# From the third expert on, the scaled routing weights are loaded and multiplied instead of multiplied and transposed

## The chip, the cores and the metric

The kernel runs on one core of one Trainium2 chip. The metric is the device time of one execution in microseconds (us). The median of three runs of the kernel before is 1072.27 us (1066.41 to 1077.67).

## What is computed

Three layers follow each other: an attention (pooled and local, added), a soft mixture of experts, and a second mixture of experts with a balanced gate. The change lies in the passage from the second to the third.

```python
# soft mixture: logits = x @ phi; slot_out comes from 8 experts with 4 slots each
c = exp(logits - logits.max(1)); c /= c.sum(1) + 1e-09
x = c @ slot_out                      # 2304 tokens x 512, from 32 slots
# second mixture, x is the x above
P = exp(x @ w_gate - max)             # 2304 x 8
for _ in range(8):                    # balanced by rows and by columns
    P /= P.sum(1, keepdims=True) + 1e-09
    P /= P.sum(0, keepdims=True) + 1e-09
    P *= N / E
out = 0
for e in range(E):                    # 8 experts, D=512, F=1024
    h = maximum(x @ w1[e], 0.0)
    out += P[:, e:e + 1] * (h @ w2[e])
```

Since x is c @ slot_out, x @ w1[e] is c @ (slot_out @ w1[e]), a product over 32 slots alone. And since P is positive, P * max(h, 0) is max(P * h, 0), so the gate of an expert can be multiplied into c before that product.

## The kernel before, in words

The 2304 tokens are 18 tiles of 128 (NT), taken in 9 pairs (NP) of 256 tokens. The program has three stages. Up to about 160 us runs the attention. From 160 to 230 us runs the soft mixture, which streams 32 weight loads of 1 MB each (tile wa, `load_wa`, L154, issued on SP's queue) past the 32 slots: the 16 of the first product (h, L712) and the 16 of the second (so, L761). After 230 us runs the second mixture, pair by pair over 8 experts in the loop at L1196; n counts its 72 pairs.

Between the two products of the soft mixture the kernel makes c: cn and rm on VectorE (L720 to L726), cr as cn/rm four times side by side on GpSimd (L729), and then `c_part` (L733) for three tiles at a time: three transposes on TensorE into PSUM (cp), a copy on ScalarE (L738), and on the upper 64 partitions the difference of exact and rounded value on VectorE (L739). So c4 holds c transposed, its high part below and its low part above. Then h1s (L746), hps (L750), hT (L755) and the second product so (L761).

In expert 0 of the second mixture the gates are computed beside the matmuls: a generator `side` (`gate`, then 8 times `sink`) is advanced by one step after every second matmul of `y_first` (L1267). A `sink` ends with five VectorE operations on cs and pg (L1146 to L1150). pg then holds the gates, 18 tiles x 8 experts.

From expert 1 on a pair consists of 84 matmuls m (`y_pair`, L1065) and 8 matmuls h (`hidden`, L971) for the pair after it. Functions are hooked to the number k of the matmul after which they are issued (`hook`, L1200). For c times gate there are two: `scale_c` (L918) at k=70 multiplies the c of pair n+4 by its gates on GpSimd into a buffer crp (two of them), with tokens on the partitions; `turn_c` (L930) at k=64 transposes the crp of pair n+3 with two TensorE transposes (cq), copies it on ScalarE into cx (L937), and takes the difference on VectorE (L938). `hidden` then reads cx.

GpSimd also makes the low parts of the activations (s, `sums`, L998) four times a pair, and the split weights of the next expert (wt, wf, w2r, `w_early` and `w_late`) from pair 4 on to pair 0 of the next expert. SP's queue issues the loads of the next expert's weights: `load_w1` (two, L815) in pair 0, `load_w2` (two, L823) in pair 3, and in the last expert the stores.

Every engine takes its instructions in the order of the program. A DMA carries one of eight completion semaphores, DMAHW0 to DMAHW7, given out in turn over the DMAs of all queues. A DMA that gets a semaphore first waits, on the queue that issues it, until the DMA that had this semaphore before has landed.

Of the kernel before, what the change touches and what calls it, by code (L numbers as in the profile page):

```python
# [50 lines left out]
def attn_moe_moe_kernel(  # L51
# [75 lines left out]
            nc.gpsimd.tensor_copy(out=mask[96:128, 2 * NSET - 2 + h, :], in_=m0[:, 2, :])  # L127


    pg = big.tile([128, NT, E], FP32, name="pg")  # L130
    soT = big.tile([128, KD, 1, NS], FP32, name="soT")
    g4 = big.tile([128, E], FP32R, name="g4")
# [546 lines left out]
    with mctx:  # L679
# [53 lines left out]
        def c_part(t):  # L733
            cp = ps.tile([128, 3, 128], FP32, name="cp", tag="s")
            for i in range(3):
                nc.tensor.transpose(cp[:, i, :], cr[:, t + i].rearrange("p g s -> p (g s)"), ident)
            cv = c4[:, 128 * t:128 * t + 384].rearrange("p (i j) -> p i j", i=3)
            nc.scalar.activation(out=cv, in_=cp, func=ACTF.Copy)  # L738
            nc.vector.tensor_tensor(  # L739
                out=cv[64:128], in0=cp[64:128], in1=cv[64:128].bitcast(FP32), op=ALU.subtract  # L740
            )

        for t in range(0, NT, 3):
            c_part(t)
# [169 lines left out]
    hl = []  # L914
    ce = {}
    crp = {}

    def scale_c(e, p):  # L918

# [10 lines left out]
    def turn_c(e, p):  # L930
        cp = xq.tile([128, 256], FP32, name="cq", tag="x")
        t = crp.pop((e, p))
        for i in range(2):
            nc.tensor.transpose(cp[:, 128 * i:128 * i + 128], t[:, 128 * i:128 * i + 128], ident)  # L934
        o = 1024 + 256 * ((e * NP + p) % 4)
        r = ce[e, p] = cx[0][:, o:o + 256]
        nc.scalar.activation(out=r, in_=cp, func=ACTF.Copy)  # L937
        nc.vector.tensor_tensor(out=r[64:128], in0=cp[64:128], in1=r[64:128].bitcast(FP32), op=ALU.subtract)  # L938

    def relu(out, ps_, in1, op1):  # L940
        nc.vector.scalar_tensor_tensor(out=out, in0=ps_, scalar=0.0, in1=in1, op0=ALU.max, op1=op1)  # L941
# [236 lines left out]
    def side_all():  # L1178
        yield from gate()
        for _ in range(8):  # L1180
            yield from sink()

    side = side_all()
    next(soon)
# [9 lines left out]
        return seq[n] if n < len(seq) else None  # L1194

    for n, (e, p) in enumerate(seq):  # L1196
        nx, nx3, nx4 = at(n + 1), at(n + 3), at(n + 4)
        hooks = {}

        def hook(k, f, *a):  # L1200
# [30 lines left out]
        if n == NP - 1:  # L1231
            for k, i in (6, 0), (11, 1), (20, 2):
                hook(k, turn_c, 1, i)
                hook(k + 2, scale_c, 1, 2 + i)
        elif n >= NP:
            if nx3:
                hook(64, turn_c, *nx3)
            if nx4:
                hook(70, scale_c, *nx4)
        if nx and nx[0] == 1:  # L1240
            hook(fr(40), scale_first, nx[1])
        if n == 3:
# [62 lines left out]
```

## Time and profile before

| what | value |
|---|---|
| median of three runs | 1072.27 us |
| profiled execution, its own time | 1071.43 us |
| its span, first to last instruction | 1069.7 us |
| mean granted TensorE clock | 0.973 |
| TensorE busy | 1018.8 us, 95% |
| VectorE / ScalarE / GpSimd busy | 780.5 / 539.1 / 649.4 us |

PE is TensorE, DVE VectorE, ACT ScalarE, POOL GpSimd, SP SyncE, which only issues DMAs (SPq is its queue). The granted clock is 1.00 at 2.4 GHz and 0.50 at 1.2 GHz. A row of the timeline has the start in us from the start of the span, the duration in us, engine, line, operation, output<-inputs, the count of merged instructions, and in brackets the idle time of the engine before it and what ended it. Matmuls overlap, so what a matmul takes of TensorE is read from the start of the next.

### The profile page before, as it was taken

To read this page: it belongs to the slowest core of one execution; us is meant where nothing else is said; L and a number is where in the kernel's file an instruction comes from. 1 tells how busy PE (TensorE), PEld (TensorE's weight loads), DVE (VectorE), ACT (ScalarE), POOL (GpSimd) and SP (SyncE) were. 2 spreads that over 40 slices of the span, in tenths; PEclk is the share of its full clock that TensorE was granted. 3 is DMA by queue.
4 is the path that set the end of the run, shared out by engine and by line. 5 is a ranking of instruction groups with operands and counts; after the bars stand their busy time and mean duration, and the time that the engine had idled before them with its cause. 6 is when DMAs were issued, how large, how long until landed. Compare 5 with 4: busy or idle time off the path is not lost.

```text
span 1069.7 us, 22765 instructions
## 1 busy us (share of the span) xinstructions
PE 1018.8 (95%) x9033; PEld 920.0 (86%) x9033; DVE 780.5 (73%) x1521; ACT 539.1 (50%) x1040; POOL 649.4 (61%) x543
## 2 busy tenths in 40 slices
PE   6887888879999999999999999999999999999998
PEld 5676653257787999999999999999999999999998
DVE  4998962145575678777878778778777788788996
ACT  4987740132224655655565456445645565455442
POOL 6655441020033957984897589658956995699452
PEclk8999978879999999999999999999999999999999
DMA  9999998961100220022003100310111022000111
GB/s 196 173 186 246 264 306 292 386 224 40 40 1 1 79 80 2 1 80 80 2 1 119 41 1 2 119 40 1 58 65 38 2 79 80 2 2 21 59 41 61
DMA packets 95919, 93.84 MB, mean 88 GB/s; under 512 B 59076, under 2 KB 64836, under 8 KB 95812
## 3 DMA queue, kind: packets, MB, share of 16 engines
q1 hardware_dynamic: 95812, 92.37, 30.1%
q8 instruction: 72, 1.18, 0.5%
q14 instruction: 35, 0.29, 0.1%
HBM read 87.64 MB, written 4.72 MB: 86 GB/s over the span
## 4 chain that ended last, share of the span: by engine, by line
PE 79%; POOL 7%; DMA 5%; DVE 3%; ACT 2%; SPq 2%; issue 1%; POOLq 0%; ACTq 0%; DVEq 0%
PE m L1065 52%; PE y L1022 9%; PE h L971 5%; POOL s L842 3%; POOL wt L842 2%; DMA kn<-in_k_dram 2%; PE ap L885 1%; PE h L712 1%; DMA w1s<-in_moe_w_dram 1%; PE cq L934 1%; DMA wa<-in_moe_w_dram 1%; PE loc L465 1%; PE h L952 1%; PE so L761 1%; SPq L222 1%
## 5 line engine op out<-in xcount | busy, mean ns | idle before, releaser
L842 POOL TENSOR_TENSOR s<-xs,s 128x512 fp32r<-128x512 f32 x252 | 323.0, 1298 | 177.5 <-ACT s L997 177.5
L1065 PE MATMUL m<-wt,s 128*128 128x256 f32 x3024 | 389.1, 280 | 1.0 <-POOL s L842 1.0
L1065 PEld LDWEIGHTS m<-wt,s 128*128 128x128 f32 x3024 | 369.5, 188 | 12.5 <-issue 10.1
L1065 PE MATMUL m<-wt,d 128*128 128x256 f32 x2268 | 289.4, 282 | 1.6 <-DVE acc L1052 1.1
L1065 PEld LDWEIGHTS m<-wt,d 128*128 128x128 f32 x2268 | 273.8, 188 | 2.2 <-PE m L1065 1.5
L1052 DVE TENSOR_TENSOR acc<-acc,m 128x512 f32<-128x512 f32 x315 | 215.2, 683 | 22.6 <-PE m L1065 9.4
L997 ACT ACTIVATE s<-xs 128x512 fp32r<-128x512 f32 x252 | 155.1, 629 | 103.8 <-DVE xs L941 93.1
L941 DVE SCALAR_TENSOR_TENSOR d<-h,d 128x768 fp32r<-128x768 f32 x126 | 120.0, 952 | 90.7 <-ACT d L1004 90.7
L1004 ACT ACTIVATE d<-h 128x768 fp32r<-128x768 f32 x126 | 102.1, 810 | 74.1 <-PE m L1065 74.0
L941 DVE SCALAR_TENSOR_TENSOR xs<-h,xs 128x256 f32<-128x256 f32 x252 | 107.0, 425 | 8.6
L941 DVE SCALAR_TENSOR_TENSOR xs<-h,r 128x256 f32<-128x256 f32 x252 | 94.6, 417 | 19.6 <-issue 11.1
L1022 PE MATMUL y<-whi,s 128*128 128x512 f32 x272 | 89.2, 406 | 1.7 <-ACT whi L835 1.7
L980 ACT ACTIVATE r<-h 128x256 f32<-128x256 f32 x126 | 48.6, 386 | 81.0 <-PE h L971 81.0
L842 POOL TENSOR_TENSOR wt<-w2r,wt 128x1024 fp32r<-128x1024 f32 x35 | 83.9, 2407 | 7.3 <-ACT wt L848 7.3
L971 PE MATMUL h<-cx,a4s 128*128 128x256 f32 x504 | 80.4, 282 | 0.0
L971 PEld LDWEIGHTS h<-cx,a4s 128*128 128x128 f32 x504 | 68.6, 189 | 0.1
L1022 PEld LDWEIGHTS y<-whi,s 128*128 128x128 f32 x272 | 50.8, 191 | 12.4 <-ACT whi L835 2.4
L842 POOL TENSOR_TENSOR wf<-w2r 128x1024 f32<-128x1024 f32 x14 | 33.8, 2413 | 42.1 <-DVE a4s L907 42.1
L965 ACT ACTIVATE s<-h 128x512 fp32r<-128x512 f32 x34 | 20.3, 598 | 72.2 <-PE h L952 54.0
L1022 PE MATMUL y<-wlo,s 128*128 128x512 f32 x136 | 55.3, 407 | 0.0
L937 ACT ACTIVATE cx<-cq 128x256 fp32r<-128x256 f32 x63 | 24.0, 381 | 58.2 <-PE cq L934 58.2
L842 POOL TENSOR_TENSOR wt<-wf,wt 128x1024 fp32r<-128x1024 f32 x14 | 33.6, 2400 | 31.7 <-ACT wt L848 31.7
(206 smaller groups left out, 1158.9 us busy)
## 6 DMA issues: line engine op xcount, KB each, us to landing
wa<-in_moe_w_dram SPq DMA_DIRECT2D x32, 1024.0 KB, 8.3
w1r<-in_moe_w_dram SPq DMA_DIRECT2D x14, 1024.0 KB
w2r<-in_moe_w_dram SPq DMA_DIRECT2D x14, 1024.0 KB, 5.3
vw<-in_v_dram SPq DMA_DIRECT2D x62, 96.0 KB, 5.1
kn<-in_k_dram SPq DMA_DIRECT2D x32, 144.0 KB, 5.8
vg<-in_v_dram SPq DMA_DIRECT2D x16, 288.0 KB
out_dram<-acc SPq DMA_DIRECT2D x18, 256.0 KB, 2.0
qn<-in_q_dram SPq DMA_DIRECT2D x20, 144.0 KB, 6.0
```

The costliest lines, as they stand in the source:

```text
L222: nc.sync.dma_start(out=vw[32 * c:32 * c + 32, lo:hi, :], in_=rows(v, b, 2 * hp, 24 * c - 4 + 96 * lo, [[D, 32], [96 * D, hi - lo], [1, D]]),)
L842: eng.tensor_tensor(out=out, in0=x, in1=y, op=ALU.subtract)
L937: nc.scalar.activation(out=r, in_=cp, func=ACTF.Copy)
L941: nc.vector.scalar_tensor_tensor(out=out, in0=ps_, scalar=0.0, in1=in1, op0=ALU.max, op1=op1)
L965: nc.scalar.activation(out=hi[:, h], in_=ps[:, j], func=ACTF.Relu)
L971: nc.tensor.matmul(out=ps[:, j, 256 * k:256 * k + 256], lhsT=a4s[:, e % 2, 128 * g:128 * g + 128], rhs=ce[e, p], start=True, stop=True,)
L980: nc.scalar.activation(out=r21, in_=A21, func=ACTF.Relu)
L997: nc.scalar.activation(out=t[:, 0], in_=v, func=ACTF.Copy)
L1004: nc.scalar.activation(out=t[:, 0], in_=H[e, p, c][0][:, :, 128:512], func=ACTF.Relu)
L1022: nc.tensor.matmul(out=ys[i], lhsT=l, rhs=r, start=(c == 0 and n == 0), stop=(c == 1 and n == 11))
L1052: nc.vector.tensor_tensor(out=v, in0=v, in1=ps, op=op_)
L1065: nc.tensor.matmul(out=ps[:, place], lhsT=l, rhs=W[e, n][:, r, j, :], start=(m == 0), stop=(m == 11))
```

## The change

The scaled c of experts 2 to 7 no longer comes from a product with tokens on the partitions that is then transposed. `c_part` keeps a copy of the transposed c: VectorE copies 32 partitions of cp into a tile cst, and a DMA on ScalarE's queue writes it to a scratch c_dram in memory. After the eight `sink`s a new last step of `side`, `keep_gates`, transposes pg on TensorE (two transposes, tile gr), copies it on VectorE, and writes it to a scratch g_dram with two DMAs on SP's queue.

For a pair of the experts 2 to 7, `load_c` then loads, at k=72 of pair n, c for pair n+5 (four DMAs of 32 partitions x 1 KB into crp, the same rows to each quarter) and the gates (one DMA, one row of memory read to all 128 partitions, into a part of lnat that is free by then), all on SP's queue. `mul_c` multiplies the two on GpSimd at k=70 of the next pair. `make_c` copies on ScalarE and takes the difference on VectorE at k=64 of the pair after, both now from SBUF. No transpose is left there. Expert 1 stays as it was.

```diff
+    c_dram = dram.tile([NS, N], FP32, name="c_dram")
+    g_dram = dram.tile([NT * E, 128], FP32, name="g_dram")
...
+            cs = mw.tile([NS, 384], FP32, name="cst", tag="cst", bufs=4)
+            nc.vector.tensor_copy(out=cs, in_=cp[0:NS].rearrange("p i j -> p (i j)"))
+            nc.scalar.dma_start(out=c_dram[:, 128 * t:128 * t + 384], in_=cs)
...
+    def load_c(e, p):
+        t = crp[e, p] = mm.tile([128, 256], FP32, name="crp", tag="crp", bufs=2)
+        g = lnat.rearrange("p t s -> p (t s)")[:, 256 * ((e * NP + p) % 2):256 * ((e * NP + p) % 2) + 256]
+        G[e, p] = g
+        for r in range(4):
+            nc.sync.dma_start(out=t[32 * r:32 * r + 32], in_=c_dram[:, 256 * p:256 * p + 256])
+        gd = g_dram[16 * p + e:16 * p + e + 1, :]
+        nc.sync.dma_start(
+            out=g.rearrange("p (i j) -> p i j", i=2),
+            in_=bass.AP(tensor=gd.tensor, offset=gd.offset, ap=[[0, 128], [128 * E, 2], [1, 128]]),
+        )
+    def mul_c(e, p):
+        t = crp[e, p]
+        nc.gpsimd.tensor_tensor(out=t, in0=t, in1=G.pop((e, p)), op=ALU.mult)
+    def make_c(e, p):
+        t = crp.pop((e, p))
+        o = 1024 + 256 * ((e * NP + p) % 4)
+        r = ce[e, p] = cx[0][:, o:o + 256]
+        nc.scalar.activation(out=r, in_=t, func=ACTF.Copy)
+        nc.vector.tensor_tensor(out=r[64:128], in0=t[64:128], in1=r[64:128].bitcast(FP32), op=ALU.subtract)
+    def keep_gates():
+        gt = xq.tile([128, 2, 128], FP32, name="gr", tag="x")
+        pv = pg.rearrange("p t e -> p (t e)")
+        nc.tensor.transpose(gt[:, 0, :], pv[:, 0:128], ident)
+        nc.tensor.transpose(gt[0:16, 1, :], pv[:, 128:144], ident)
+        yield
+        gs = op.tile([128, 2, 128], FP32, name="r21", tag="r21", bufs=2)
+        nc.vector.tensor_copy(out=gs[:, 0, :], in_=gt[:, 0, :])
+        nc.vector.tensor_copy(out=gs[0:16, 1, :], in_=gt[0:16, 1, :])
+        yield
+        nc.sync.dma_start(out=g_dram[0:128, :], in_=gs[:, 0, :])
+        nc.sync.dma_start(out=g_dram[128:144, :], in_=gs[0:16, 1, :])
+        yield
...
+        yield from keep_gates()
...
-                hook(64, turn_c, *nx3)
+                hook(64, turn_c if nx3[0] == 1 else make_c, *nx3)
             if nx4:
-                hook(70, scale_c, *nx4)
+                hook(70, scale_c if nx4[0] == 1 else mul_c, *nx4)
+            if nx5 and nx5[0] > 1:
+                hook(72, load_c, *nx5)
```

Three places show how the instructions move. The first is `c_part` on ScalarE's queue; before, six copies stand there in one row:

```order
L738 ACTIVATE c_2681<-cp 128x384 [waits PE_49] x6
L747 ACTIVATE h1s<-h_2712 128x512 [waits DVE_49]
```

Now a DMA stands behind each copy (the first three of six are shown). It waits for VectorE's copy of cp and for one of the eight semaphores:

```order
L741 ACTIVATE c_2685<-cp 128x384 [waits PE_49]
L747 DMA c_dram<-cst 32x384 [waits DMAHW1_49,DVE_49]
L741 ACTIVATE c_2685<-cp 128x384 [waits PE_49]
L747 DMA c_dram<-cst 32x384 [waits DMAHW3_49,DVE_49]
L741 ACTIVATE c_2685<-cp 128x384 [waits PE_49]
L747 DMA c_dram<-cst 32x384 [waits DMAHW5_49,DVE_49]
```

The same place on SP's queue, the fourth to the eighth of the 16 weight loads wa of the second product. Before, the semaphores of the weight loads follow each other:

```order
L163 DMA wa<-in_moe_w_dram 128x4x512 [waits DMAHW1_49,PE_49]
L163 DMA wa<-in_moe_w_dram 128x4x512 [waits DMAHW2_49,PE_49]
L163 DMA wa<-in_moe_w_dram 128x4x512 [waits DMAHW3_49,PE_49]
L163 DMA wa<-in_moe_w_dram 128x4x512 [waits DMAHW4_49,PE_49]
L163 DMA wa<-in_moe_w_dram 128x4x512 [waits DMAHW5_49,PE_49]
```

Now (the fourth to the eleventh load) the six writes of c_dram have taken semaphores 1, 3, 5, 6, 0 and 2 between them:

```order
L166 DMA wa<-in_moe_w_dram 128x4x512 [waits DMAHW2_49,PE_49]
L166 DMA wa<-in_moe_w_dram 128x4x512 [waits DMAHW4_49,PE_49]
L166 DMA wa<-in_moe_w_dram 128x4x512 [waits DMAHW7_49,PE_49]
L166 DMA wa<-in_moe_w_dram 128x4x512 [waits DMAHW1_49,PE_49]
L166 DMA wa<-in_moe_w_dram 128x4x512 [waits DMAHW3_49,PE_49]
L166 DMA wa<-in_moe_w_dram 128x4x512 [waits DMAHW4_49,PE_49]
L166 DMA wa<-in_moe_w_dram 128x4x512 [waits DMAHW5_49,PE_49]
L166 DMA wa<-in_moe_w_dram 128x4x512 [waits DMAHW6_49,PE_49]
```

So the seventh load (the fourth row) carries semaphore 1, which the first write of c_dram had before it; the eighth load carries that of the second write, the tenth and the eleventh those of the third and the fourth, and the thirteenth and the fifteenth those of the last two.

The second place is TensorE in expert 0, behind the last `sink`. Before, the matmuls y of `y_first` and four h run on:

```order
L952 MATMUL h<-c_2681,a4s 128x256 x4
L1022 MATMUL y<-wlo,s_3666 128x512
L1022 MATMUL y<-whi,s_3666 128x512
L1022 MATMUL y<-whi,s_3667 128x512
L1022 MATMUL y<-wlo,s_3666 128x512
```

Now the two transposes of the gates (gr) stand after the second y behind the h, with a wait for VectorE, which writes pg:

```order
L998 MATMUL h<-c_2685,a4s 128x256 x4
L1068 MATMUL y<-wlo,s_3688 128x512
L1068 MATMUL y<-whi,s_3688 128x512
L975 MATMUL gr<-ident,pg 128x128 [waits DVE_49,PE_49]
L976 MATMUL gr<-ident,pg 16x128
L1068 MATMUL y<-whi,s_3689 128x512
L1068 MATMUL y<-wlo,s_3688 128x512
```

The third place is a pair of expert 2 or later on VectorE. Before, cx is the difference of cq, which is in PSUM:

```order
L1052 TENSOR_TENSOR acc<-acc,m 128x2x256 [waits DVE_49,PE_49] x2
L938 TENSOR_TENSOR cx<-cq,cx 64x256 [waits Activation_49]
L941 SCALAR_TENSOR_TENSOR d<-h,d 128x768 [waits Activation_49]
L1052 TENSOR_TENSOR acc<-acc,m 128x2x256 [waits DVE_49,PE_49]
```

Now it stands at the same position with both inputs in SBUF:

```order
L1098 TENSOR_TENSOR acc<-acc,m 128x2x256 [waits DVE_49,PE_49] x2
L969 TENSOR_TENSOR cx<-crp,cx 64x256 [waits DMAHW4_49,DMAHW3_49,Activation_49]
L987 SCALAR_TENSOR_TENSOR d<-h,d 128x768 [waits Activation_49]
L1098 TENSOR_TENSOR acc<-acc,m 128x2x256 [waits DVE_49,PE_49]
```

## Rows read from the trace of the kernel before

**Rows 1.** The page: busy us of each engine, share of the span, instructions.
```profile
PE 1018.8 (95%) x9033; PEld 920.0 (86%) x9033; DVE 780.5 (73%) x1521; ACT 539.1 (50%) x1040; POOL 649.4 (61%) x543
```

**Rows 2.** Timeline of TensorE, two pairs of expert 3.
```profile
567.30 0.38 PE L934 MATMUL cq<-ident,crp 128*128 128x128 f32 x2
567.44 2.58 PE L1065 MATMUL m<-wt,d 128*128 128x256 f32 x20
...
578.28 0.38 PE L934 MATMUL cq<-ident,crp 128*128 128x128 f32 x2
```

**Rows 3.** The chain that ended last, in order of time: start, us, engine, group.
```profile
418.58 2.36 POOL wt L842
...
466.27 1.68 PE m L1065 x12
```

**Rows 4.** Timeline of all engines, `c_part` and the start of so.
```profile
188.47 0.87 ACT L738 ACTIVATE c<-cp 128x384 fp32r<-128x384 f32 x2 [13.71 <-PE cp L736]
188.99 1.03 DVE L739 TENSOR_TENSOR c<-cp,c 64x384 fp32r<-64x384 f32 x2 [12.14 <-ACT c L738]
192.44 1.04 DVE L739 TENSOR_TENSOR c<-cp,c 64x384 fp32r<-64x384 f32 x2 [0.69 <-ACT c L738]
```

**Rows 5.** Timeline of SP's queue: fourth and fifth load wa of the second product; the seventh.
```profile
175.91 0.92 SPq L163 DMA_DIRECT2D wa<-in_moe_w_dram  x2
178.09 0.81 SPq L163 DMA_DIRECT2D wa<-in_moe_w_dram  x1
```

**Rows 6.** Windows: us, busy us (instructions) of PE, PEld, DVE, ACT, POOL, clock, DMA share, GB/s.
```profile
176.00:178.00 2.00, 2.00 (x24) 0.80 (x20) 0.81 (x2) 0.00 (x0) 1.77 (x2) 1.00 0.51 96
176.00:186.00 10.00, 10.00 (x97) 3.96 (x91) 0.81 (x2) 0.00 (x0) 4.99 (x4) 1.00 0.91 320
186.00:228.70 42.70, 32.91 (x222) 13.77 (x217) 8.73 (x21) 6.74 (x14) 0.00 (x0) 0.81 1.05 387
```

**Rows 7.** The line of the stores: ns of an issue min/median/max, and us to landing.
```profile
L1089 SPq DMA_DIRECT2D out_dram<-acc x18: 332/347/375, 980.4 to 1066.1; - x18
DMA to landing us min/median/max: 2.0/2.0/2.0
```

**Rows 8.** Timeline of TensorE, the end of so and the start of the second mixture.
```profile
212.68 1.06 PE L761 MATMUL so<-wa,hT 128*32 128x512 f32 x8 [0.67 <-DMA wa<-in_moe_w_dram]
215.39 1.07 PE L761 MATMUL so<-wa,hT 128*32 128x512 f32 x8 [1.64 <-DMA wa<-in_moe_w_dram]
220.81 1.94 PE L885 MATMUL ap<-w1s,soT 128*32 128x512 f32 x8 [1.28 <-DMA w1s<-in_moe_w_dram]
```

**Rows 9.** Timeline of all engines, the last `sink` beside the weight splits of expert 1.
```profile
318.57 2.22 DVE L1149 TENSOR_TENSOR pg<-pg,cs 128x144 f32<-128x144 f32 x1
320.70 2.40 POOL L842 TENSOR_TENSOR w2r<-wf,w2r 128x1024 f32<-128x1024 f32 x1
320.82 2.37 DVE L1150 TENSOR_SCALAR pg<-pg 128x144 f32<-128x144 f32 x1
```

**Rows 10.** Timeline of TensorE, the place of the new transposes.
```profile
319.17 0.63 PE L1022 MATMUL y<-whi,s 128*128 128x512 f32 x2
```

**Rows 11.** Windows around an idle stretch of TensorE in the attention, columns as in rows 6.
```profile
101.00:103.50 2.50, 0.09 (x1) 0.12 (x2) 0.19 (x1) 0.89 (x3) 2.15 (x4) 1.00 0.97 205
103.50:107.00 3.50, 3.50 (x36) 3.25 (x38) 2.16 (x4) 1.40 (x3) 1.67 (x2) 0.52 0.91 195
```

**Rows 12.** Lines L842 (DVE) and L923 (POOL): ns min/median/max, first and last start.
```profile
L842 DVE TENSOR_TENSOR acc<-acc x18: 424/427/1368, 976.7 to 1065.7; 128x256 f32<-128x256 f32 x18
L923 POOL TENSOR_TENSOR crp<-lnat,pg x64: 605/619/811, 336.7 to 1021.5; 128x256 f32<-128x256 f32 x64
```

**Rows 13.** Timelines of GpSimd, VectorE and TensorE, expert 2's end.
```profile
559.22 0.96 DVE L941 SCALAR_TENSOR_TENSOR d<-h,d 128x768 fp32r<-128x768 f32 x1 [1.57 <-ACT d L1004]
...
567.87 5.04 POOL L842 TENSOR_TENSOR s<-xs,s 128x512 fp32r<-128x512 f32 x4
...
569.86 0.40 PE L1065 MATMUL m<-wt,s 128*128 128x256 f32 x2
```

More of the change, by code (lines that the diff above doesn't have):

```diff
@@ L127, in make_masks @@
             nc.gpsimd.tensor_copy(out=mask[96:128, 2 * NSET - 2 + h, :], in_=m0[:, 2, :])
+    dram = ctx.enter_context(tc.tile_pool(name="dram", bufs=1, space=bass.MemoryType.DRAM))
+    c_dram = dram.tile([NS, N], FP32, name="c_dram")
+    g_dram = dram.tile([NT * E, 128], FP32, name="g_dram")
     pg = big.tile([128, NT, E], FP32, name="pg")
@@ L916, in attn_moe_moe_kernel @@
     crp = {}
+    G = {}
     def scale_c(e, p):
@@ L1196, in attn_moe_moe_kernel @@
     for n, (e, p) in enumerate(seq):
-        nx, nx3, nx4 = at(n + 1), at(n + 3), at(n + 4)
+        nx, nx3, nx4, nx5 = (at(n + i) for i in (1, 3, 4, 5))
         hooks = {}
```

## The prediction

> **What bounds the kernel now.** Read the busy times first: TensorE is busy 95% of the span, no other engine over 73% [rows 1]. The shares mix the stages, so the chain that ended last comes next. From 466 us to the end it names TensorE alone; there a pair of experts 2 to 7 takes 10.98 us, from one cq to the next, with no gap between matmuls [rows 2]. Just before, from 418.58 to 466.27 us, it names GpSimd [rows 3]: at the end of expert 1 its splits and low parts are the limit. The third view is the stage before 230 us, by windows: from 186 to 228.7 us the DMA engines move 387 GB/s without a pause [rows 6], and TensorE waits at the end of so and at ap for what they bring [rows 8]. So there are three limits: DMA until the second mixture starts, GpSimd for 48 us, and TensorE. The change touches all three.
>
> The profiled execution took 1071.43 us (span 1069.7), 0.84 below the median of the three runs, whose spread is 11 us. The sum is made against 1071.43.
>
> **The transposes go.** Two cq per pair, for 54 pairs. They start at 567.30 and the next m starts at 567.44, so the two take 0.14 us of TensorE, though they are listed with 0.38 [rows 2]. 54 x 0.14 = 7.6 us, all of it on the path where TensorE is the limit: **-7.6 us**.
>
> The Trainium skill, page "TensorE: Matmul & The Clock Gate" (Part 4: PE-mode transpose), gives about 275 ns for a transpose in a kernel. One after another, 108 of them would be 29.7 us by that. This trace differs: they overlap with their neighbours, 0.07 us each from start to start.
>
> **The writes of c hold up the weight loads.** Each DMA on ScalarE's queue waits for VectorE's copy of its three tiles. The chain to the first: ScalarE's copy starts at 188.47, VectorE's difference at 188.99 and takes 0.52 (1.03 for two); the copy to cst, 384 columns too, I put at the same 0.52, so the DMA is issued at about 190.1 [rows 4]. A store lands 2.0 us after its issue [rows 7]: 192.1, say 192.2. The seventh load of so waits on SP's queue for exactly that landing, by its semaphore, and all loads behind it wait in the queue. Before, it was issued at 178.09 [rows 5].
>
> What the DMA engines still have is the fourth to sixth load, 3 x 1.05 = 3.15 MB; from 176 to 186 us they moved 10 x 320 GB/s = 3.2 MB [rows 6], so they run dry at 186.0. How soon does a load run after its issue? The fourth was issued at 175.91 [rows 5], and by 178.0 two us at 96 GB/s had moved 0.19 MB [rows 6], 0.5 us at the full rate: as if it began at 177.5, 1.6 us after the issue. So the engines resume at 192.2 + 1.6 = 193.8 and lose 7.8 us. The other writes (five of 49 KB, 0.25 MB at 387 GB/s) add 0.6. The later waits cost nothing: a write follows about every 1.9 us (copy, difference, copy to cst, issue of 0.35 [rows 7], and hand-overs), a load takes 1.05 MB / 387 GB/s = 2.7 us. Since no pause follows in which the loss could be made up before 228.7, so's last weights and w1s, for which TensorE waits [rows 8], come later by all of it: **+8.4 us**.
>
> `c_part` itself also grows, from 0.86 us for three tiles ((192.44 - 188.99) / 4 [rows 4]) to about 1.9, so h1s starts some 6.2 us later (six times 1.04). Alone that would cost less: so has waits of 0.67 and 1.64 us to give and ap 1.28 [rows 8], together 3.6, so 2.6 would be left. It runs under the 8.4 and isn't added; if the semaphore wait is gone, it is the price.
>
> **The gates wait behind VectorE.** The new transposes stand behind the first y of the row at 319.17, so TensorE reaches them at 319.40 [rows 10]. They need pg, and its last operation ends at 320.82 + 2.37 = 323.19: VectorE's short operations on cs and pg there each wait until GpSimd's running split of 2.4 us is over [rows 9]. Before, nothing but ScalarE and VectorE waited for this. TensorE takes its matmuls in order, and the y behind can't pass: 3.8 us, and 0.14 for the transposes. An idle stretch of this size also lowers the clock: after 2.5 us with 0.09 busy the granted clock was 0.52 for 3.5 us though TensorE was busy [rows 11], so half of 3.4 us goes too, 1.7. **+5.6 us** (3.9 if the clock holds).
>
> **The new work of a pair.** `mul_c` has the size of `scale_c`, 619 ns [rows 12], and takes its place: nothing. `make_c` on ScalarE stands where the copy of cq stood and waits for less. On SP, five DMAs at 0.35 us are 1.8 us of a queue with 10.8 us a pair; `load_c` waits there for `make_c` of two pairs earlier, in step with TensorE, and gives mul_c some 8 us. The load_w2 behind it is issued up to 7 us later in pair 2 and still a pair ahead of its first use. load_w1 in pair 0 waits for GpSimd as before, and the c loads behind its 2 MB (5.4 us) land some 3 to 4 us ahead of mul_c.
>
> VectorE's difference now has both inputs in SBUF, and that is new in these pairs. The nearest row: acc<-acc with all in SBUF takes 427 ns, but up to 1368 beside GpSimd [rows 12], and the operations of rows 9 wait to the end of GpSimd's instruction. So the difference will wait, up to 2.4 us. Behind it stands d, which waits 1.57 us for ScalarE anyway [rows 13], so VectorE hides most of it. GpSimd in turn waits for the difference. A bound from below is nothing, from above its 0.43; I take 0.3.
>
> The Trainium skill, "SBUF — State Buffer" (SBUF: two separate sides), calls this an exclusive lock, held for the whole instruction by whichever starts first, a VectorE operation with two SBUF inputs or GpSimd; the loser fully blocks. The trace agrees for VectorE [rows 9]; what GpSimd loses no row shows alone. By that rule it is the whole 0.43 in each of 54 pairs, the upper bound.
>
> Where GpSimd is the limit [rows 3], four pairs (n=15 to 18) give it 4 x 0.3 = 1.2, and TensorE's 4 x 0.14 = 0.6 there is not gained: **+1.8 us**. At the other five ends of an expert GpSimd runs late by several us: the first s for the next pair ends at about 567.87 + 1.26 = 569.13, and TensorE needs it at its second m, 569.86 + 0.12 [rows 13]: 0.85 us to spare. Two waits of 0.3 in the two pairs ahead and three pairs shorter by 0.14 take 1.0: 0.2 short, five times: **+1.0 us**.
>
> **Sum.** 1071.4 - 7.6 + 8.4 + 5.6 + 1.8 + 1.0 = 1080.6; I say **1081 us**, 0.9% over 1071.4. A measurement of this kernel can tell about 1% from no change, so this is at the edge.
>
> **Rivals.** *The writes hold nothing up.* If a write is in memory much earlier, or SP's wait were already satisfied, the price is c_part's 2.6 instead of 8.4: 1081 - 5.8 = 1075. Against it speaks the order of the program: the seventh load can't be issued before a value that only exists after 187 us. Chance 0.13.
>
> *The transposes were worth more.* With 275 ns each the gain would be 29.7 instead of 7.6: 1081 - 22 = 1059, faster. The start of the next m speaks against it [rows 2]. Chance 0.02.
>
> *GpSimd becomes the limit at the end of every expert: slower.* It has 0.85 us to spare at a boundary [rows 13]. If it loses the whole 0.43 in each of the pairs 4 to 8 and 0, as its pairs with two splits leave it almost nothing idle, it comes 6 x 0.43 + 3 x 0.14 = 3.0 late and TensorE waits 2.2 at each of six boundaries instead of 0.2: some 10 us more, 1091. It decides from 0.85 us of accumulated delay on. Against it: a pair with one s waiting for ScalarE resets the delay. With half of it, 1086. Chance 0.22. The c loads coming late behind load_w1 would look alike from TensorE (GpSimd waits for DMA in pair 1); they are in this chance.
>
> **Chances and range.** The forecast as worked out holds 0.63; its own range is 1077 to 1085 (the clock holds: 1079; the writes land 2 us sooner or later: 1079 or 1083; the lock at 0 or 0.43). With the first rival below and the middle of the third above, eight in ten lie from 1073 to 1088. Slower by over 1% begins at 1083: a quarter of the forecast's own chance (0.16) and the third rival (0.22), with what is unnamed 0.40. Faster by over 1% ends at 1061: the second rival, 0.02. The rest, 0.58, is within 1%.
>
> **What would show it.** The seventh load's issue near 192 with DMA idle before it, and so's last wait near 224; TensorE idle for 3.8 us ahead of gr with VectorE's pg as releaser, and the clock at 0.5 behind it; pairs of 10.84 us in experts 2 to 7; the difference on VectorE (cx<-crp,cx) at means of 1 us or more; GpSimd's s as TensorE's releaser at the ends of experts. It is wrong if the DMA engines don't pause, if gr's wait is short because the splits and the last `sink` no longer meet, or if pairs lose their 0.14 to new waits.

## The result and the profile after

The changed kernel takes 1083.36 us (median of 14 executions), the kernel before 1071.43 beside it: a ratio of 1.0128, with a 95% interval of 1.0103 to 1.0152, so 13.7 us slower. The forecast was 1081, its range 1073 to 1088. The total fell into the range, but several of its terms were wrong in size, the wait at the end of expert 1 by most, and their errors partly cancel.

The busy times of after, to be held against [rows 1]:

```profile
span 1085.0 us, 23175 instructions
PE 1015.6 (94%) x8927; PEld 912.5 (84%) x8927; DVE 817.1 (75%) x1529; ACT 535.1 (49%) x1040; POOL 664.9 (61%) x543
```

TensorE has 3.2 us less to do, VectorE 36.6 us more. The span is 15.3 us longer (1085.0 against 1069.7). To see where, I set the starts of a few instructions of TensorE in the two traces side by side: the first cp, the first y, and the first h of a pair of experts 1 to 7 (h0 is the first of expert 1; from h7 to h61 lie the 54 pairs that lost their transposes).

| piece | before, us | after, us | difference | forecast |
|---|---|---|---|---|
| start to first cp (attention, unchanged) | 187.88 | 188.54 | +0.66 | 0 |
| first cp to first y (soft mixture) | 41.42 | 51.58 | +10.16 | +8.4 |
| first y to h0 (expert 0, gates) | 111.82 | 117.78 | +5.96 | +5.6 |
| h0 to h8 (one of the 54 pairs) | 92.17 | 91.95 | -0.22 | -0.1 |
| h8 to h12 (four of them, end of expert 1) | 45.62 | 52.33 | +6.71 | +1.2 |
| h12 to h54 (42 of them, four expert ends) | 477.87 | 470.36 | -7.51 | -5.1 |
| h54 to h62 (seven of them, expert 7) | 87.64 | 87.63 | -0.01 | -0.8 |
| h62 to the end | 25.28 | 24.83 | -0.45 | 0 |

The forecast of a piece is the prediction's terms spread over it: -0.14 for each of its pairs, +1.8 at the end of expert 1, +0.2 at each other expert's end.

**The soft mixture.** The places of [rows 5] and [rows 6], after: first the sixth to eighth weight load of so in SP's timeline.

```profile
178.28 0.37 SPq L166 DMA_DIRECT2D wa<-in_moe_w_dram  x1
...
192.45 0.37 SPq L166 DMA_DIRECT2D wa<-in_moe_w_dram  x1
...
197.47 0.37 SPq L166 DMA_DIRECT2D wa<-in_moe_w_dram  x1
```

Then the windows of the same stretch (busy time and count of each engine, granted clock, share of the DMA engines, GB/s):

```profile
186.00:192.00 6.00, 3.94 (x35) 1.67 (x25) 1.38 (x3) 0.98 (x2) 0.00 (x0) 1.00 0.07 18
192.00:196.00 4.00, 1.40 (x6) 0.81 (x6) 2.15 (x5) 0.98 (x2) 0.00 (x0) 0.77 0.55 177
196.00:202.00 6.00, 1.14 (x5) 0.77 (x5) 3.70 (x7) 1.27 (x3) 0.00 (x0) 0.50 0.78 227
202.00:210.00 8.00, 7.41 (x36) 4.22 (x40) 0.42 (x1) 0.31 (x1) 0.00 (x0) 0.50 1.03 394
```

The seventh load is issued at 192.45 (forecast 192.2; 178.09 before), and the DMA engines move 18 GB/s until 192, where they had moved 386. The first packets of a load move again at 193.47 (forecast 193.8), but a second pause follows: the eighth load is issued only at 197.47, and no packet of a load starts from 197.19 to 198.46. The packets and semaphore counts in the trace show what it waited for. The second write, issued at 192.88 just behind the seventh load, did not move before 196.26 and landed at 197.41, 4.5 us after its issue; the first, on idle DMA engines, had landed after 1.6 us. So the windows from 192 to 202 have only 177 and 227 GB/s. Counted at 388 GB/s, 5.7, 2.2 and 2.5 us are lost in the three windows, 10.4 together, about the +10.16.

**The gates.** VectorE's last operations on pg, and TensorE behind them (timelines of after; the brackets are the idle time ahead and what ended it):

```profile
327.59 2.07 DVE L1193 TENSOR_SCALAR cs<-cs 128x8 f32<-128x8 f32 x1
329.93 2.19 DVE L1195 TENSOR_TENSOR pg<-pg,cs 128x144 f32<-128x144 f32 x1
332.16 2.31 DVE L1196 TENSOR_SCALAR pg<-pg 128x144 f32<-128x144 f32 x1
...
334.62 0.45 PE L975 MATMUL gr<-ident,pg 128*128 128x128 f32 x1 [3.69 <-DVE pg L1196]
```

The window behind gr, for the granted clock (the third number from the end):

```profile
334.00:337.50 3.50, 2.88 (x8) 2.36 (x9) 2.14 (x5) 0.60 (x1) 0.38 (x1) 0.52 0.00 0
```

Operations on 8 and 144 elements a partition take over 2 us, as in [rows 9], and TensorE waits 3.69 us (forecast 3.8); the granted clock is 0.52 in the 3.5 us from 334.0 on, as the forecast took it for 3.4 us.

**A pair of experts 2 to 7.** The place of [rows 2], where a pair took 10.98 us:

```profile
548.51 0.64 PE L1017 MATMUL h<-cx,a4s 128*128 128x256 f32 x4
...
554.84 4.36 PE L1111 MATMUL m<-wt,d 128*128 128x256 f32 x36
559.04 0.40 PE L1111 MATMUL m<-wt,s 128*128 128x256 f32 x2
559.27 0.64 PE L1017 MATMUL h<-cx,a4s 128*128 128x256 f32 x4
```

559.27 - 548.51 = 10.76 us: the pair is 0.22 shorter, not 0.14.

**The end of expert 1.** The chain that ended last, of after, from 459 us on (start, duration, what):

```profile
459.93 8.76 DVE cx L969
...
468.70 0.97 DVE d L987
469.67 0.04 issue
469.72 1.23 PE h L1017 x4
```

GpSimd's timeline of the same stretch:

```profile
459.16 2.42 POOL L848 TENSOR_TENSOR w2r<-wf,w2r 128x1024 f32<-128x1024 f32 x1
461.52 1.46 POOL L848 TENSOR_TENSOR acc<-acc 128x256 f32<-128x256 f32 x2
462.91 2.50 POOL L848 TENSOR_TENSOR s<-xs,s 128x512 fp32r<-128x512 f32 x2
465.35 2.36 POOL L848 TENSOR_TENSOR wt<-wf,wt 128x1024 fp32r<-128x1024 f32 x1
467.65 0.74 POOL L962 TENSOR_TENSOR crp<-crp,lnat 128x256 f32<-128x256 f32 x1
472.59 1.28 POOL L848 TENSOR_TENSOR s<-xs,s 128x512 fp32r<-128x512 f32 x1 [4.20 <-ACT s L1043]
```

Before, the chain of this stretch named GpSimd from 418.58 to 466.27 [rows 3]. Now it names TensorE up to 455 us, and then VectorE: one difference of 64 partitions x 256 stands in the trace for 8.75 us. None of the semaphores that it waits for is GpSimd's (the third place under "The change"). GpSimd was running when it came, and went through seven instructions without a gap. The difference ended 0.29 us after the last of them (467.65 + 0.74 = 468.39, against 468.68). Then GpSimd itself had nothing to do: its next s needs xs, which VectorE had not made. TensorE waited 6.57 us for d, which stands behind the difference on VectorE, and from 467.3 to 474.1 us the granted clock was 0.50:

```profile
469.72 1.23 PE L1017 MATMUL h<-cx,a4s 128*128 128x256 f32 x4 [6.57 <-DVE d L987]
```

### The profile page after: what moved, and what is told of

Read it like the earlier page. It is cut to its first block, busy times and chain, and to the rows that moved or that the text cites. A ratio compares the mean times of both kernels' runs of the same rounds, so it can differ in the third digit from the quotient of the medians.

```text
span 1085.0 us, 23175 instructions
## 1 busy us (share of the span) xinstructions
PE 1015.6 (94%) x8927; PEld 912.5 (84%) x8927; DVE 817.1 (75%) x1529; ACT 535.1 (49%) x1040; POOL 664.9 (61%) x543
## 4 chain that ended last, share of the span: by engine, by line
PE 76%; DVE 3%; POOL 2%; DMA 1%; ACT 1%; issue 0%; ACTq 0%; DVEq 0%
PE m L1111 56%; PE y L1068 9%; PE h L1017 5%; PE ap L891 2%; PE h L715 2%; DMA wa<-in_moe_w_dram 1%; POOL wt L848 1%; PE h L998 1%; DVE cx L969 1%; POOL s L848 1%; PE as L907 1%; PE so L767 1%; PE sip L614 0%; PE hps L756 0%; DVE xs L987 0%
## 5 line engine op out<-in xcount | busy, mean ns | idle before, releaser
L848 POOL TENSOR_TENSOR s<-xs,s 128x512 fp32r<-128x512 f32 x252 | 328.3, 1319 | 160.9 <-ACT s L1043 159.7
L1111 PE MATMUL m<-wt,d 128*128 128x256 f32 x2268 | 278.9, 280 | 1.0 <-DVE acc L1098 0.9
L1111 PEld LDWEIGHTS m<-wt,d 128*128 128x128 f32 x2268 | 270.7, 188 | 2.5 <-PE m L1111 1.5
L969 DVE TENSOR_TENSOR cx<-crp,cx 64x256 fp32r<-64x256 f32 x54 | 56.7, 1049 | 3.5 <-ACT cx L968 2.0
```

The source lines that it names most:

```text
L848: eng.tensor_tensor(out=out, in0=x, in1=y, op=ALU.subtract)
L969: nc.vector.tensor_tensor(out=r[64:128], in0=t[64:128], in1=r[64:128].bitcast(FP32), op=ALU.subtract)
L1111: nc.tensor.matmul(out=ps[:, place], lhsT=l, rhs=W[e, n][:, r, j, :], start=(m == 0), stop=(m == 11))
```

## The experiments

Each kernel was run beside the kernel before; ratios are to before. The attention stage, which nothing here touches, differs from one profiled execution to the next (the first cp comes between 182.9 and 190.0 us), so for a single effect I compare the pieces of the table. Each kernel has one profiled execution: a long wait that its trace shows, or lacks, need not be so in the others.

**1. The front alone.** The experts build c as before; only the writes of c and the gates' transposes stay.

```diff
-                hook(64, turn_c if nx3[0] == 1 else make_c, *nx3)
+                hook(64, turn_c, *nx3)
-                hook(70, scale_c if nx4[0] == 1 else mul_c, *nx4)
+                hook(70, scale_c, *nx4)
-            if nx5 and nx5[0] > 1:
-                hook(72, load_c, *nx5)
```

> The writes of c and of the gates stay as changed, but all experts build c as before (scaled on GpSimd, turned on TensorE); nothing reads the scratch. Theory: TensorE's first h of expert 1 comes 16.8 us later than before (357.9 against 341.1 in the two traces), and nothing behind it differs, so the whole is 16.8 us over before: ratio to before 1.0157, 1.5 us over the changed kernel (15.3 over before in its trace). Then the new work of a pair gains 1.5 us net. Rival: part of the 16.8 us is idle time that the experts would have had anyway, or the new pairs cost more than they give; then this kernel is no slower than the changed one: 8 to 15 us over before.

Ratio 1.0176 (1.0133 to 1.0218). First cp to first y 51.82 us, first y to h0 118.62, and from h0 to h62 703.29, where before has 703.30 and the changed kernel 702.27. So the loss of the front is a loss of its own, all of it in the time, and the whole rework of the pairs gained 1.0 us between h0 and h62.

**2. The writes behind so.** VectorE's copies go into one tile, and two DMAs write it when so is done.

```diff
-            cs = mw.tile([NS, 384], FP32, name="cst", tag="cst", bufs=4)
-            nc.vector.tensor_copy(out=cs, in_=cp[0:NS].rearrange("p i j -> p (i j)"))
-            nc.scalar.dma_start(out=c_dram[:, 128 * t:128 * t + 384], in_=cs)
+            q, u = t // 9, 128 * (t % 9)
+            nc.vector.tensor_copy(
+                out=cst[32 * q:32 * q + 32, u:u + 384], in_=cp[32 * q:32 * q + 32].rearrange("p i j -> p (i j)")
+            )
...
         nc.vector.tensor_copy(out=soT[:, :, 0, :], in_=sop)
+        for q in range(2):
+            nc.scalar.dma_start(out=c_dram[:, 1152 * q:1152 * q + 1152], in_=cst[32 * q:32 * q + 32])
```

> The changed kernel, but VectorE's copies of c are gathered in one tile and written in two DMAs behind the product so, so that no load of so's weights waits for the landing of a write; the copies in c_part stay. Theory: the wait of the loads for the landing is the cause of the pause of the DMA engines; the seventh load is issued near 178 us again, the pause from 186 to 192 is gone, and the first y comes 10.1 us earlier less what c_part's growth costs by itself (2.6 by the forecast): 6 to 10 us under the changed kernel, about 1075. Rival: c_part, which is 6 us longer, delays hps and so by itself, and the pause of the DMA engines was hidden under it: 0 to 3 us under the changed kernel.

Ratio 1.0008 (0.9983 to 1.0034): 1.2% less than the changed kernel, more than expected. The windows show no pause:

```profile
186.00:192.00 6.00, 2.42 (x12) 1.43 (x12) 5.34 (x11) 1.96 (x4) 0.00 (x0) 0.78 1.05 387
192.00:196.00 4.00, 2.95 (x14) 2.95 (x15) 0.98 (x2) 0.60 (x1) 0.00 (x0) 0.50 1.05 387
196.00:202.00 6.00, 5.41 (x28) 1.73 (x31) 0.42 (x1) 0.00 (x0) 0.00 (x0) 0.50 1.05 387
```

First cp to first y takes 40.12 us (51.58 in the changed kernel, 41.42 before). The copies in `c_part` are still there, and yet nothing of the 2.6 us that I had priced for them is lost. So starts 13.41 us after the first cp instead of 9.15 before, 4.3 later (the price stood on 6.2), but then it runs without a wait for weights:

```profile
197.27 16.77 PE L770 MATMUL so<-wa,hT 128*32 128x512 f32 x128 [0.59 <-DVE hT L764]
```

The waits that so and ap had before [rows 8] covered what `c_part` grew. The chain that ended last shows it: before, it named the load of w1s from 206.07 us for 14.70 us; here it names so and the work behind it. The rival falls, and so does my 2.6.

The stage is 11.5 us shorter than in the changed kernel; another 2.2 came off between the first y and h0 (115.57 against 117.78). TensorE waits for gr as long as there, but the granted clock does not fall:

```profile
317.59 0.30 PE L980 MATMUL gr<-ident,pg 128*128 128x128 f32 x1 [3.69 <-DVE pg L1201]
```

```profile
317.50:321.00 3.50, 3.41 (x16) 2.83 (x17) 2.31 (x5) 0.60 (x1) 0.00 (x0) 1.00 0.07 20
```

**3. The same writes from another queue.** To separate the semaphores from the writes: the six DMAs stand where the change put them, on GpSimd's queue. In the trace they carry six semaphores that no load of SP's queue carries, so the eight are handed round over SP's and ScalarE's queues, and not over all.

```diff
-            nc.scalar.dma_start(out=c_dram[:, 128 * t:128 * t + 384], in_=cs)
+            nc.gpsimd.dma_start(out=c_dram[:, 128 * t:128 * t + 384], in_=cs)
```

> The changed kernel with the six writes of c issued in the same place of the program, but from GpSimd's queue, whose transfers count on semaphores of their own. The data written, the copies and their times stay. Theory: the weight loads waited for the landing of the writes by the semaphores that both queues share in turn; here the seventh load is issued 6 us before the first cp again, the DMA engines don't pause, and from the first cp to the first y it takes 40 to 42 us instead of 51.6: 9 to 11 us under the changed kernel. Rival: the writes themselves, or c_part's length, hold the stage up; then the stage stays over 48 us.

Ratio 1.0047 (1.0026 to 1.0067), 0.8% less than the changed kernel, and first cp to first y 40.69 us. The writes, issued from 189.4 to 196.5, land after 4.7 to 5.0 us, and no load waits for them; VectorE waits once, 1.2 us, at a copy to cst. SP's timeline, with the seventh load and the two behind it, and a window:

```profile
177.11 0.46 SPq L166 DMA_DIRECT2D wa<-in_moe_w_dram  x1
...
178.37 2.88 SPq L166 DMA_DIRECT2D wa<-in_moe_w_dram  x2
```

```profile
186.00:192.00 6.00, 3.19 (x27) 1.64 (x18) 3.81 (x7) 1.85 (x4) 1.41 (x3) 1.00 1.04 386
```

The seventh load leaves SP's queue at 177.11, 9.8 us ahead of the first cp of this execution (186.91), as before the change (178.09 and 187.88), and before any write exists. With the same bytes written at the same place of the program, only the semaphores shared with the loads are gone, and with them the 10 us. This settles that term.

**4. The gates ten steps later.**

```diff
+        for _ in range(10):
+            yield
         yield from keep_gates()
```

> The changed kernel, with ten more steps (about ten y, 4.7 us) between the last operation on pg and the transposes of the gates. Theory: the transposes then find pg ready, TensorE's wait of 3.69 us ahead of gr and the granted clock of 0.50 to 0.57 behind it are gone: 5 to 6 us under the changed kernel, about 1078. Rival: the wait is that of VectorE for GpSimd's splits and comes back at the new place, or the later place delays the first scaled c of expert 1: within 2 us of the changed kernel.

Ratio 1.0076 (1.0041 to 1.0111), 0.5% less than the changed kernel. First y to h0 is 112.49 us (117.78 changed, 111.82 before), and gr now follows the y without a wait:

```profile
333.41 0.39 PE L1068 MATMUL y<-wlo,s 128*128 128x512 f32 x1
333.64 0.27 PE L975 MATMUL gr<-ident,pg 128*128 128x128 f32 x1
333.75 0.27 PE L976 MATMUL gr<-ident,pg 128*16 128x128 f32 x1
333.77 0.72 PE L1068 MATMUL y<-whi,s 128*128 128x512 f32 x2
```

5.3 us were the wait and the clock behind it; 0.7 are left for the transposes and what else `side` now does.

**5. VectorE's first input from PSUM.** ScalarE copies the upper rows of c to the bank that cq had, and the difference reads them there.

```diff
         r = ce[e, p] = cx[0][:, o:o + 256]
+        cp = xq.tile([128, 256], FP32, name="cq", tag="x")
+        nc.scalar.activation(out=cp[64:128], in_=t[64:128], func=ACTF.Copy)
         nc.scalar.activation(out=r, in_=t, func=ACTF.Copy)
-        nc.vector.tensor_tensor(out=r[64:128], in0=t[64:128], in1=r[64:128].bitcast(FP32), op=ALU.subtract)
+        nc.vector.tensor_tensor(out=r[64:128], in0=cp[64:128], in1=r[64:128].bitcast(FP32), op=ALU.subtract)
```

> The changed kernel, but ScalarE first copies rows 64 to 127 of c to PSUM (a bank that the old cq held), and VectorE's difference takes its first input from there, as before the change; GpSimd's product, the loads and the scratch stay. Theory: VectorE's wait of 8.75 us at 459.93 (and 0.65 to 1.33 us per difference elsewhere) comes from both inputs lying in SBUF beside a busy GpSimd; here the difference takes 0.43 us, the pair 9 to 10 at the end of expert 1 is no longer 7.9 us longer than before but at most 2, the pairs of expert 7 fall from 10.94 to 10.76 us: 7 to 10 us under the changed kernel, about 1075. Rival: GpSimd's product of 0.74 us in place of 0.61 is what makes the end of expert 1 later; then the gain is under 2 us. ScalarE's extra copy, about 0.3 us a pair, is hidden by both.

Ratio 1.0074 (1.0041 to 1.0108), 0.5% less than the changed kernel and a little less than expected. h8 to h12 is 46.12 us (52.33 changed, 45.62 before), so the loss at the end of expert 1 was VectorE's wait and not GpSimd's longer product. The groups of the two kernels, changed and this one:

```profile
L969 DVE TENSOR_TENSOR cx<-crp,cx 64x256 fp32r<-64x256 f32 x54 | 56.7, 1049 | 3.5 <-ACT cx L968 2.0
```

```profile
L971 DVE TENSOR_TENSOR cx<-cq,cx 64x256 fp32r<-64x256 f32 x54 | 23.1, 428 | 8.4 <-ACT cx L970 6.6
```

The profiled execution is the slowest of this kernel's nine (1086.45 us, median 1077.05), and its trace has a new long wait in expert 7 (timelines of VectorE, GpSimd and TensorE):

```profile
987.05 6.03 DVE L848 TENSOR_TENSOR acc<-acc 128x256 f32<-128x256 f32 x1
993.11 0.43 DVE L971 TENSOR_TENSOR cx<-cq,cx 64x256 fp32r<-64x256 f32 x1
...
987.08 5.04 POOL L848 TENSOR_TENSOR s<-xs,s 128x512 fp32r<-128x512 f32 x4
992.03 0.78 POOL L962 TENSOR_TENSOR crp<-crp,lnat 128x256 f32<-128x256 f32 x1
...
994.59 1.22 PE L1019 MATMUL h<-cx,a4s 128*128 128x256 f32 x4 [3.79 <-DVE d L989]
```

Another VectorE instruction with both inputs in SBUF, the acc that finishes an output, met four s and the product in a row, and waited 6.03 us until GpSimd had nothing more. Here too h is 3.8 us late, the granted clock is 0.50 from 993.4 to 1000.2, and the pair takes 17.37 us. It is an instruction that stood in the kernel before too, where it took up to 1.37 us [rows 12]. One other execution took 1084.49 us and seven took 1073 to 1078, so most of them seem to be without this wait; no trace shows that.

**6. That input alone, on the kernel before.** From expert 2 on ScalarE puts the turned c back to SBUF, and nothing else is changed.

```diff
+        x = cp
+        if e > 1:
+            x = t
+            nc.scalar.activation(out=x[64:128], in_=cp[64:128], func=ACTF.Copy)
-        nc.vector.tensor_tensor(out=r[64:128], in0=cp[64:128], in1=r[64:128].bitcast(FP32), op=ALU.subtract)
+        nc.vector.tensor_tensor(out=r[64:128], in0=x[64:128], in1=r[64:128].bitcast(FP32), op=ALU.subtract)
```

> The kernel before, with one part of the change alone: from expert 2 on ScalarE puts rows 64 to 127 of the turned c back into crp in SBUF and VectorE's difference reads both inputs there. No scratch, no loads, GpSimd's product as before. Theory: that alone makes VectorE wait for GpSimd: the difference takes 0.65 to 1.4 us instead of 0.43 at the ends of experts, and one at the end of expert 1 may wait up to 9 us (it did in four of five kernels with SBUF inputs, 1.9 in the fifth), so the span from the pair 8 to the pair 12 is 47 to 53 us instead of 45.6, the two pairs at the start of the other experts are a few tenths longer: 1 to 8 us over before. Rival: without the loads and the longer product GpSimd leaves gaps at the right time, VectorE never waits over more than one of its instructions, and the time is within 1 us of before.

Ratio 1.0053 (1.0021 to 1.0085). In the profiled execution, the slowest of ten (1078.77 us, median 1073.88), h8 to h12 is 51.97 us, 6.35 more than before. One instruction stands out, at the same end of expert 1 though a pair earlier:

```profile
431.51 7.63 DVE L942 TENSOR_TENSOR cx<-crp,cx 64x256 fp32r<-64x256 f32 x1 [0.86 <-ACT crp L941]
```

Neither the loads nor the new product nor the missing transposes are in this kernel. Where the input lies is enough for the wait.

**7. Late writes and late gates together.** The edits of 2 and 4.

> Late writes and late gates together, the difference still with both inputs in SBUF beside GpSimd. Theory: the front costs nothing any more (cp to first h of expert 1 within 1 us of before), the experts take what they took in the changed kernel (702 us from the first h to the last pair, 703.3 before): the same as before within 0.3%, ratio 0.996 to 1.000. The wait of 7 to 9 us at the end of expert 1 stays. Rival: that wait was brought by the delay of the front and goes with it; then the ratio is near 0.990.

Ratio 0.9964 (0.9935 to 0.9992), as expected; the front is neutral (first cp to h0 152.77 us, 153.24 before). But the long wait, which I expected to stay, is not in the profiled execution: h8 to h12 is 46.96 us. VectorE and GpSimd at the place in question:

```profile
439.03 1.92 DVE L974 TENSOR_TENSOR cx<-crp,cx 64x256 fp32r<-64x256 f32 x1 [0.49 <-ACT cx L973]
...
438.27 2.40 POOL L853 TENSOR_TENSOR w2r<-wf,w2r 128x1024 f32<-128x1024 f32 x1
440.62 1.64 POOL L853 TENSOR_TENSOR acc<-acc 128x256 f32<-128x256 f32 x2
```

Here the difference got in after one GpSimd instruction (its end is 440.95; w2r ended at 440.67), though the next followed at once. It waited 8 to 9 us in the profiled executions of the changed kernel and of experiments 2, 3 and 4, and 7.6 in experiment 6. That the delay of the front brings the wait (the rival) is refuted by experiment 6, which has it without that delay (first cp to h0 153.35 us); in experiment 2, which has it too, 2.4 us of the delay are left. What decides between one instruction and all of them isn't shown by these traces. It may differ between executions of one kernel: the profiled one took 1061.03 us, and this kernel's twelve reach from 1058.53 to 1074.54.

**8. All three edits**, those of 2, 4 and 5.

> All three edits at once: writes of c behind so, gates ten steps later, VectorE's first input in PSUM. Theory: the three losses are separate and add up. Against before: from the first cp to the first y 1.3 us less (as with the late writes), from there to the first h of expert 1 0.7 more (as with the late gates), and from that h to the last pair 3.7 less if one 6 us wait of VectorE's acc in expert 7 stays (699.6 against 703.3), 10 less if not: 1058 to 1064 on the median of before, ratio 0.990 to 0.996. Rival: DMA, GpSimd or VectorE gives one of the gains back once the others are gone; then the ratio is 0.997 or more.

Ratio 0.9890 (0.9856 to 0.9923). First cp to first y 39.76, first y to h0 112.77, h0 to h62 694.14: the parts add up, and a 6 us wait in expert 7 did not come in this execution.

**9. All three, and the finishing differences on GpSimd** in expert 7, but for the last pair.

```diff
-                    sub(nc.vector, av[:, R], av[:, V], av[:, R])
+                    sub(nc.vector if p == NP - 1 else nc.gpsimd, av[:, R], av[:, V], av[:, R])
...
-                    sub(nc.vector, av[:, Q], av[:, V], av[:, Q])
+                    sub(nc.vector if p == NP - 1 else nc.gpsimd, av[:, Q], av[:, V], av[:, Q])
```

> As all three edits at once, and in expert 7 the two differences that finish a pair's output (acc from acc and acc, both in SBUF) go to GpSimd for all pairs but the last, so that no VectorE instruction of that stretch has two inputs in SBUF. Theory: the wait of 6.03 us of acc at 987 and the one of TensorE behind it (3.8 us and its clock) are gone, the experts take 693 us: ratio 0.988 to 0.990 to before, 5 to 7 us under the kernel with the three edits if that still has the wait. Rival: GpSimd, with 1.4 us more per pair of expert 7, is late with s; then the pairs of expert 7 are longer than 10.76 us and nothing is gained.

1055.59 us, ratio 0.9875 (0.9852 to 0.9899): the lowest median of the kernels here, 14 us under the 1069.70 of before beside it. The pairs of expert 7 take 10.76 us. Windows of a pair each, of the changed kernel and then of this one:

```profile
1016.58:1027.51 10.93, 10.93 (x94) 10.82 (x93) 10.42 (x19) 4.90 (x10) 5.97 (x6) 1.00 0.22 72
```

```profile
975.61:986.38 10.77, 10.77 (x95) 10.77 (x93) 8.62 (x16) 5.63 (x11) 7.91 (x9) 1.00 0.22 74
```

In the changed kernel VectorE is busy 10.42 of 10.93 us of such a pair: there it had become the limit, with the difference at 0.85 us beside the acc at 1.06. Against the kernel with the three edits alone the intervals overlap, so that the last edit helps is shown in the trace (86.21 us from h54 to h62, against 86.57) and not in the times.

**10. Four transposes instead of two**, on the kernel before, from expert 2 on; the second two repeat the first two.

```diff
-        for i in range(2):
+        for i in (0, 1) * (2 if e > 1 else 1):
```

> The kernel before, with the two transposes of each pair from expert 2 on done twice into the same place (four in a row). Theory: what the two cost is not the 0.14 us between the first one's start and the next m's but the whole lengthening of the pair, 0.22 us (10.98 against 10.76), of which 0.08 is paid once per group for the change to other work and back; two more in the same group then cost 0.14 again and a pair takes 11.12. Rival: each transpose costs 0.11 us by itself, and the pair takes 11.20. Over 54 pairs 7.6 or 11.9 us.

Ratio 1.0153 (1.0097 to 1.0210); in the trace 11.5 us more from the first cp to the end. A pair takes 11.20 us (567.83 - 556.63), the rival's number and not the theory's 11.12:

```profile
562.95 2.03 PE L1065 MATMUL m<-wt,d 128*128 128x256 f32 x16
564.82 0.60 PE L934 MATMUL cq<-ident,crp 128*128 128x128 f32 x4
565.18 2.58 PE L1065 MATMUL m<-wt,d 128*128 128x256 f32 x20
567.60 0.40 PE L1065 MATMUL m<-wt,s 128*128 128x256 f32 x2
```

Four transposes take 0.36 us to the next m and lengthen the pair by 0.44 over the pair without any; two took 0.14 and lengthened it by 0.22. So each costs 0.11 us, and the start of the next m is 0.08 too early a mark: the matmuls behind it run late by the rest (565.18 to 567.60 is 2.42 us for 20 m, which at 4.20 / 36 need 2.33).

## Why the prediction was right, and where it was not

**The transposes: too small.** The prediction took 0.14 us a pair from the start of the first cq to the start of the next m, 7.6 in all. It is 0.22, 11.9 over 54 pairs (experiment 10). The step that failed is the reading of the cost from the next start alone, the rule given above the rows: the difference of whole pairs, which the trace of before had beside it (10.98 us with two transposes, 10.76 in a pair without any, from 1033.66 to 1044.42), would have given it. The rival of 275 ns each, from the Trainium skill's page "TensorE: Matmul & The Clock Gate" (Part 4: PE-mode transpose), stays off as a cost: one transpose is listed with 0.27 us in the rows of experiment 4, but what it adds to the pair is 0.11.

**The writes: right in kind, too small by 1.8.** The place (the seventh load), its time (192.45, forecast 192.2) and the dry DMA engines came as worked out, and experiments 2 and 3 show the semaphores as the cause. The step that failed is "the later waits cost nothing", which compared a write every 1.9 us with a load of 2.7 us and let each write land as soon as the first. But the first landing lets the seventh load out, and the second write, issued 0.4 us behind that load, lands with the end of it (197.41; the load at 197.63). Only then is the eighth load issued, at 197.47, so the stream pauses a second time. The price for `c_part`'s length alone, 2.6, was also wrong: it stood on 6.2 us of growth where so starts 4.3 and 5.0 us later in experiments 2 and 3, and in both the stage is a little shorter than before (40.12 and 40.69 us against 41.42). The waits for weights took up 3.6 of the growth, and the clock gave time back too: in the last 9 us ahead of the first y it was 0.50 before and 1.00 in both experiments.

**The gates: right in this execution.** 3.69 us of wait and a clock of 0.52 behind it; +5.96 against +5.6, and 5.3 of it vanish with ten steps more (experiment 4). The clock's part, 1.7, did not follow from the idle time alone: behind the same 3.69 us the granted clock was 0.50 for 3.3 us here, for 6.6 in experiment 1, and never fell in experiment 2, where first y to h0 cost 3.75 over before, near the 3.9 given for a clock that holds.

**The lock: seen, and mis-sized where it counts.** The prediction said that the difference will wait "up to 2.4 us", one GpSimd instruction, and let d's own wait for ScalarE hide most of it. In 53 of 54 pairs the wait stayed within that: they took 1.53 us at most, (56.7 - 8.75) / 53 = 0.91 in the mean. In one pair it waited for seven, 8.75 us, longer than all that could hide it, and the end of expert 1 cost 7.6 us over what the shorter pairs gave there (6.71 + 4 x 0.22) instead of 1.8. The Trainium skill, "SBUF — State Buffer" (SBUF: two separate sides), has the loser blocked for the other's whole instruction. The trace agrees for those 53; in the one pair VectorE was blocked for a whole run of seven instructions. The charge was also put on the wrong engine: the sum let GpSimd lose 0.3 us a pair and be the limit, while experiment 5, with GpSimd's work as in the changed kernel, gets back 6.2 of the 6.7 us. The third rival stood nearest (loss at the expert ends, by the lock), but its mechanism, GpSimd late at each boundary, is not what the trace shows.

**The other expert ends: 0.2 forecast for each, 0.4 measured.** The two pairs around an end take 11.03 to 11.05 and 10.95 to 11.00 us instead of 10.76, about 0.5 together; from h12 to h54 four ends cost -7.51 + 42 x 0.22 = 1.7. With the difference from PSUM the first of them falls to 10.76 and the second to about 10.9.

**Expert 7: not in the prediction.** Its pairs were to gain 0.14 each and gained nothing (87.63 against 87.64), because VectorE, with two acc more per pair there, became the limit: with the difference at 0.43 us instead of 0.85, all but one of them fall to 10.76 (experiment 5). VectorE, busy for 95% of such a pair after, would have asked for a sum of its own.

Summed against the forecast of 9.2 us more than before: writes +1.8, gates +0.4, end of expert 1 +5.8 (7.6 - 1.8), the other four ends +0.9 (1.7 - 0.8), expert 7 +1.3 (1.5 lost, 0.2 forecast), attention and last pairs, which the change does not touch, +0.2, transposes -4.3: 6.1 together, the 15.3 us of the two profiled executions. By the ratio the kernel is 13.7 us slower, 4.5 more than forecast. So it is in part luck that the number came near: the largest error, the wait at the end of expert 1, was mostly paid for by transposes that were worth more than I took them for.

## What to carry to other kernels

A DMA added on one engine's queue can stop the loads of another, where both draw on the same completion semaphores: look up which later load gets the semaphore of the new DMA, and put the DMA behind those loads, or on a queue with semaphores of its own. A VectorE instruction with two inputs in SBUF beside a GpSimd that runs without gaps can wait for the whole run of GpSimd and not for one instruction of it, so the run is the upper bound of its price; one input in PSUM avoided it, at the price of a copy on a ScalarE that had room. And what a few short matmuls cost is read from the whole period with and without them, not from the next start.

## What the runs showed of the hardware that was not expected

- A VectorE instruction with both inputs in SBUF waited 8.75 us through seven GpSimd instructions, and ended 0.29 us after GpSimd ran out of work; 6.03 and 7.63 us in two other kernels. In one execution the like instruction got in after a single one (1.92 us). What decides that stays open.
- With one input in PSUM the same difference took 428 ns in the mean of 54, at the same places.
- Six writes of 49 KB cost 10 us, as loads behind them waited for their landing: the first landed 1.6 us after its issue, the second, issued behind a load of 1 MB, after 4.5 us. From GpSimd's queue they landed after 4.7 to 5.0 us and cost nothing.
- Behind the same idle 3.69 us of TensorE the granted clock was 0.50 for 3.3 us, for 6.6 us, or did not fall, in three kernels. What decides that stays open.
- A transpose of 128x128 among matmuls costs 0.11 us of TensorE's time, though the next matmul starts only 0.07 us later per transpose.
